# Projecting two heads through a block-diagonal omega instead of two row-packed halves

## The chip, the cores and the metric

The kernel runs on one core of a Trainium2 chip. The metric is the device time of one execution in microseconds (us), lower is better. A profile of one execution lists every instruction of the five engines: TensorE as two rows, PE for matmuls and PEld for the weight loads that go with them, VectorE (DVE), ScalarE (ACT), GpSimd (POOL) and SyncE (SP), which issues most DMAs. In the trace a matmul in full fp32 stands as two records (96 matmuls of a line give 192 records), one in fp32r as one record. The end of a matmul record is modelled, so blocks are measured here from start to start.

## What is computed

Random-feature attention on 4 batches, 8 heads, 576 tokens of 64 channels, 128 features, followed by a mixture of four experts:

```python
def phi(x):
    proj = np.einsum('bhsd,md->bhsm', x, omega)
    sq = np.sum(x * x, axis=-1, keepdims=True) / 2.0
    h = proj - sq
    h = h - np.max(h, axis=-1, keepdims=True)
    return np.exp(h) / np.sqrt(m)
q_p, k_p = (phi(q_s), phi(k_s))
kv = np.einsum('bhsm,bhsd->bhmd', k_p, v)
z = np.sum(k_p, axis=2)
num = np.einsum('bhsm,bhmd->bhsd', q_p, kv)
den = np.einsum('bhsm,bhm->bhs', q_p, z)[..., None] + 1e-06
x = num / den                              # 2304 tokens of 512 channels
for e in range(4):
    out += p[:, e:e + 1] * (np.maximum(x @ w1[e], 0.0) @ w2[e])
```

## The kernel before

One core does everything in one program whose order is written out by hand. Batch 0 is attended first (`class Pair`). The experts' work is cut into visits (a part of the tokens with half an expert): `plain` visits, then `fast` visits, which save products by sums and differences of blocks. While TensorE works through visits, the attention of batches one to three is fed in between in small ticks (`later_ticks`): 12 pairs of heads, each an object of `class Halves`. The last eight visits (`DEEP`) save products in the second layer too (`sevens`).

A pair of heads has its keys in one SBUF tile `k` of 128 partitions by 2 by 576: half 0 (`t[:, 0]`) holds the keys transposed, channels of head 0 on partitions 0 to 63 and of head 1 on 64 to 127; half 1 (`kn`) holds the same keys by tokens, which POOL squares in place (`square`, L251) and DVE sums to lengths (`lengths`, L255). Queries go the same way in a tile `q`. `om_r` holds omega transposed and scaled, 64 by 128, once for each head: on partitions 0 to 63 and again on 64 to 127.

`project` (L266) makes the features of 512 of the 576 tokens. For each of four groups of 128 tokens it does one matmul per head: the tokens are the stationary operand, 64 partitions by 128 columns, omega the moving one, 64 by 128. The two heads use different halves of the array's rows, and write to different PSUM banks (`ps[0]`, `ps[1]`). `project_tails` (L274) does the same for the last 64 tokens of each head, one matmul per head, to two banks more. Then come the row maxima (`maxima`, `maxima_tails`), the bias, and the exponentials on ACT. `sum_keys` multiplies the keys' features by the values: nine matmuls over the full array in fp32, one with 256 moving columns (L310) and eight with 128 (L314). `turn` transposes the queries' features (L325, L329), `numerators` (L353 to L355) applies the sums.

PSUM has eight banks, given out in turn by `bank`. In the `DEEP` visits `start_sides2` begins the work on the next visit's second-layer weights: four additions on POOL (L547 to L550, tile `w2f`). For the first `DEEP` visit it stands inside `sevens`, behind the splitting of `r11` on POOL (L956, then L502 `t_hl<-r`).

Of the kernel before, what the change touches and what calls it, by code (L numbers as in the profile page):

```python
# [6 lines left out]
F32 = mybir.dt.float32  # L7
F32R = mybir.dt.float32r
AF = mybir.ActivationFunctionType
ALU = mybir.AluOpType  # L10
AX = mybir.AxisListType
# [3 lines left out]
def attention_moe(ctx, tc, kT, qT, kd, qd, kn, qn, vn, omT, probs, w1, w2, out):  # L15
# [10 lines left out]
    nc = tc.nc  # L26
    _, NP, D, _ = kT.shape
    B, S = vn.shape[:2]
    M = omT.shape[1]
    NT, DM = out.shape  # L30
    E, FP, P, _ = w1.shape
# [9 lines left out]
    const = ctx.enter_context(tc.tile_pool(name="const", bufs=1))  # L41
# [24 lines left out]
    def bank(name):  # L66
        return psum.tile([P, 512], F32, tag="ps", name=name)
# [3 lines left out]


    om = const.tile([P, M], F32, name="om")
    om_r = const.tile([P, M], F32, name="om_r")
    ident = const.tile([P, P], F32, name="ident")
    pr = const.tile([P, NT // P, E], F32, name="pr")
    prs = const.tile([P, NT // P], F32, name="prs")
# [1 line left out]
    va = const.tile([P, 4, VZ], F32, name="va")  # L79
# [24 lines left out]
    H = 2 * P  # L104

    def held(shape, tag, dtype=F32R, name=None):
        return moe.tile(shape, dtype, tag=tag, name=name or tag, bufs=BUFS[tag])
# [5 lines left out]
    class Pair:  # L113
# [7 lines left out]
        def load(self, which, eng=nc.sync):  # L121
            src = {"k": kT, "q": qT}[which[0]][self.b, self.hp][:, TILES[int(which[1])]]
            t = xop([P, src.shape[1]], which, F32)
            setattr(self, which, t)
            eng.dma_start(t[:D], src)
# [28 lines left out]
        def exp(self, which, g):  # L154
            ps, nm = getattr(self, f"{which}h{g}")
            n = len(GROUPS[g])
            size = "t" if n == 1 else ""
            if which == "k" and n > 1 or which == "q" and g == 0:
                f = held([P, n, M], "hh" if which == "k" else "hl", F32, which + "p")
            else:  # L160
                f = att.tile([P, n, M], F32, tag=which + "p" + size, name=which + "p", bufs=2)
            for i in range(n):
                nc.scalar.activation(f[:, i], ps[:, i * P:(i + 1) * P], AF.Exp, bias=nm[:, i:i + 1])
            (self.kp if which == "k" else self.qx)[g] = f
# [73 lines left out]
    class Halves(Pair):  # L238
# [4 lines left out]
        def load(self, which):  # L243
            t = att.tile([P, 2, S], F32, tag=which, name=which, bufs=1)
            for i, (name, src) in enumerate(((which, {"k": kd, "q": qd}), (which + "n", {"k": kn, "q": qn}))):
                setattr(self, name, t[:, i])
                nc.sync.dma_start(t[:, i], src[which][self.b - 1, self.hp])

        def square(self, which):
# [8 lines left out]
        def project(self, which):  # L258

            t = getattr(self, which)  # L260
            ps = [bank(which + "_ps") for _ in range(2)]
            setattr(self, which + "_ps", ps)
            for i in range(4):
                for j in range(2):
                    rows, c = slice(j * D, (j + 1) * D), i * P + (1 - j) * D
                    nc.tensor.matmul(ps[j][:, i * P:(i + 1) * P], t[rows, c:c + P], om_r[rows], start=True, stop=True)  # L266

        def project_tails(self, which):
            self.t_ps = [bank("t_ps") for _ in range(2)]
            for x in ("mx", "nb"):  # L270
                setattr(self, x + which, att.tile([P, 9], F32, tag=x + which, name=x + which))
            for j in range(2):
                rows, cs = slice(j * D, (j + 1) * D), slice(j * (S - P), j * (S - P) + P)
                nc.tensor.matmul(self.t_ps[j][:, :M], getattr(self, which)[rows, cs], om_r[rows], start=True, stop=True)  # L274

        def maxima(self, which):
            mx, ps = getattr(self, "mx" + which), getattr(self, which + "_ps")
            for j in range(2):
                nc.vector.tensor_reduce(mx[:, 4 * j:4 * j + 4], ps[j].rearrange("p (i m) -> p i m", m=M), AX.X, ALU.max)

        def maxima_tails(self, which):
            for j in range(2):
                rows = slice(j * D, (j + 1) * D)
                nc.vector.tensor_reduce(getattr(self, "mx" + which)[rows, 8:], self.t_ps[j][rows, :M], AX.X, ALU.max)

        def bias(self, which):

# [1 line left out]
            nc.vector.scalar_tensor_tensor(mx, sq, -QS * QS / 2, mx, ALU.mult, ALU.add)  # L289
            nc.vector.scalar_tensor_tensor(nb, sq, -QS * QS / 2, mx, ALU.mult, ALU.subtract)  # L290

        def exp(self, which, j):
            ps, nb = getattr(self, which + "_ps")[j], getattr(self, "nb" + which)
            f = att.tile([P, 4, M], F32, tag=which + "p", name=which + "p", bufs=2)
            for i in range(4):
                nc.scalar.activation(f[:, i], ps[:, i * P:(i + 1) * P], AF.Exp, bias=nb[:, 4 * j + i:4 * j + i + 1])
            (self.kp if which == "k" else self.qx)[j] = f

        def exp_tails(self, which):
            f = att.tile([P, 1, M], F32, tag=which + "pt", name=which + "p", bufs=2)  # L300
            for j in range(2):
                rows = slice(j * D, (j + 1) * D)
                nc.scalar.activation(f[rows, 0], self.t_ps[j][rows, :M], AF.Exp, bias=getattr(self, "nb" + which)[rows, 8:])
            (self.kp if which == "k" else self.qx)[2] = f

        def sum_keys(self):


            kv = bank("kv")[:, :VZ]
            nc.tensor.matmul(kv, self.kp[2][:, 0], vb[:, self.hp], start=True, stop=False)  # L310
            for j in range(2):
                cs = slice((1 - j) * P, (2 - j) * P)
                for t in range(4):
                    nc.tensor.matmul(kv[:, cs], self.kp[j][:, t], va[:, t, cs], start=False, stop=(j == 1 and t == 3))  # L314
            self.kv_h, self.kv_l = (att.tile([P, VZ], F32R, tag=x, name=x, bufs=1) for x in ("kvh", "kvl"))
            nc.scalar.activation(self.kv_h, kv, AF.Copy, scale=1.0 / M)
            nc.vector.scalar_tensor_tensor(self.kv_l, kv, 1.0 / M, f32(self.kv_h), ALU.mult, ALU.subtract)

        def turn(self, part):

            n = 2 * P + part * D
            ps = bank("qt_ps")
            for j in range(2):
                for t in range(2):
                    nc.tensor.transpose(ps[:, (2 * j + t) * P:(2 * j + t + 1) * P], self.qx[j][:, 2 * part + t], ident)  # L325
            pieces = [(ps.rearrange("p (j t) -> p j t", j=2), slice(0, 2 * P))]
            if part:
                pt = bank("qt_ps")[:, :P]
                nc.tensor.transpose(pt, self.qx[2][:, 0], ident)  # L329
                pieces.append((pt.rearrange("p (j t) -> p j t", j=2), slice(2 * P, 2 * P + D)))  # L330
            qt_h, qt_l = (
                att.tile([P, 2, n], F32R, tag=f"{x}1" if part else "qt", name=x, bufs=2 - part) for x in ("qth", "qtl")
            )
            for src, cs in pieces:
                nc.scalar.activation(qt_h[:, :, cs], src, AF.Copy)
                nc.vector.tensor_tensor(qt_l[:, :, cs], src, f32(qt_h[:, :, cs]), ALU.subtract)
            if part == 0:
                self.qt = {}
            self.qt[part] = qt_h, qt_l
# [134 lines left out]
    DEEP = range(N0 + NV, len(visits))  # L474
# [22 lines left out]
    def split(t, a, c, hi, lo):  # L497
        if hi is nc.scalar:
            hi.activation(a, t, AF.Copy)  # L499
        else:  # L500
            hi.tensor_copy(a, t)
        lo.tensor_tensor(c, t, f32(a), ALU.subtract)  # L502
# [294 lines left out]
    def start_sides2(v):  # L797
        B = {}
        g = w2_sides(v, B)
        next(g)  # L800
        sides2[v] = B, g
# [5 lines left out]
    def fast(v):  # L807
# [119 lines left out]
        def sevens():  # L927
# [32 lines left out]
            for q in QS3:  # L960
                seventh(q, X[q][:, R], sums_of(5), mixed(1, R), start=False)
            split(r11, *T[7], nc.scalar, nc.gpsimd)
            if v == DEEP[0]:
                start_sides2(v + 1)
            next(ready, None)
            less(t1[:, 0], first_rows(P_[1]["p1"]), t2[:, 0])
            for q in QS3:
# [16 lines left out]
            ps = bank("g2")  # L984
# [62 lines left out]
        if deep:  # L1047
            less(t1[:, 1], last_rows(P_[0]["p5"]), r11[:, 1])
            p6(1)
            split(t1, *T[5], nc.scalar, nc.gpsimd)  # L1050
            next(ready, None)
            yield from sevens()
            return
# [26 lines left out]
    def begin():  # L1080
# [6 lines left out]
        ps = [Pair(0, hp) for hp in range(NP)]  # L1087
# [17 lines left out]
        def ones_b(t):  # L1105
            nc.gpsimd.memset(t, 0.0)
            nc.gpsimd.memset(t[:D, :, P + D:], 1.0)
            nc.gpsimd.memset(t[D:, :, :D], 1.0)
# [4 lines left out]

        ones_a(va)
        ones_b(vb)
        ps[0].load_tails()
        ps[1].load_v()
        scale_om()
# [56 lines left out]
        for p in ps:  # L1175
            p.load("q1")
        for j in range(2):
            nc.sync.dma_start(om_r[j * D:(j + 1) * D], omT)

        keys_exp(3)  # L1180
        ps[2].sum_keys()
# [181 lines left out]
```

## Time and profile before

| what | value |
|---|---|
| median of 3 runs | 897.58 us (897.53 to 898.04) |
| the profiled execution | 896.99 us, of which the span from first to last instruction is 895.2 us |
| PE, PEld, DVE, ACT, POOL busy | 99%, 89%, 65%, 53%, 59% of the span |
| chain that ended last | 94% PE |
| TensorE clock granted | 1.00 throughout |
| fp32 projections L266 and L274 | 384 and 96 records in 24 blocks (12 pairs, keys and queries), 83.7 to 521 us |

The profiled execution is 0.6 us below the median, so a difference found in its rows is added to the median as it is. The busy shares name PE as the engine to look at. A busy PE is not yet a PE at its peak: it matters which records follow each other at which distance, and whether something was waited for in between.

### The profile page before, as it was taken

To read this page: it belongs to the slowest core of one execution; us is meant where nothing else is said; L and a number is where in the kernel's file an instruction comes from. 1 tells how busy PE (TensorE), PEld (TensorE's weight loads), DVE (VectorE), ACT (ScalarE), POOL (GpSimd) and SP (SyncE) were. 2 spreads that over 40 slices of the span, in tenths; PEclk is the share of its full clock that TensorE was granted. 3 is DMA by queue.
4 is the path that set the end of the run, shared out by engine and by line. 5 is a ranking of instruction groups with operands and counts; after the bars stand their busy time and mean duration, and the time that the engine had idled before them with its cause. 6 is when DMAs were issued, how large, how long until landed. Compare 5 with 4: busy or idle time off the path is not lost.

```text
span 895.2 us, 14533 instructions
## 1 busy us (share of the span) xinstructions
PE 886.4 (99%) x5340; PEld 792.5 (89%) x5340; DVE 577.5 (65%) x985; ACT 478.2 (53%) x1077; POOL 532.1 (59%) x476
## 2 busy tenths in 40 slices
PE   9999999999999999999999999999999999999998
PEld 8888888888888888889888889888989999999998
DVE  5655566776768655574766564776756856856757
ACT  5454677676774555545455445454444544544541
POOL 4756365555634453343444333558889889898883
PEclk9999999999999999999999999999999999999999
DMA  7674454444522634234334413165333334234212
GB/s 181 161 213 141 136 159 136 152 149 136 179 63 59 237 93 171 83 118 142 135 111 149 143 63 141 60 198 202 125 110 128 121 103 144 89 125 155 81 59 83
DMA packets 57447, 117.21 MB, mean 131 GB/s; under 512 B 9824, under 2 KB 19744, under 8 KB 57376
## 3 DMA queue, kind: packets, MB, share of 16 engines
q1 hardware_dynamic: 52528, 99.21, 35.0%
q0 software_dynamic: 4608, 16.78, 5.4%
q8 instruction: 42, 0.69, 0.3%
q10 hardware_dynamic: 240, 0.30, 0.1%
q14 instruction: 29, 0.24, 0.1%
HBM read 94.77 MB, written 21.50 MB: 130 GB/s over the span
## 4 chain that ended last, share of the span: by engine, by line
PE 94%; DVE 3%; POOL 1%; issue 1%; DMA 1%; ACT 1%; SPq 0%; DVEq 0%; ACTq 0%
PE g L853 28%; PE g L925 13%; PE g L680 10%; PE g L682 10%; PE g L681 10%; PE g L665 3%; PE g L667 3%; PE g L666 3%; PE kv L314 2%; PE q_ps L266 1%; PE k_ps L266 1%; PE qt_ps L325 1%; PE nd L353 1%; PE k_ps L148 1%; PE kv L178 1%; PE nd L355 1%
## 5 line engine op out<-in xcount | busy, mean ns | idle before, releaser
L502 POOL TENSOR_TENSOR w2l<-w2r,w2h 128x512 fp32r<-128x512 f32 x93 | 121.5, 1316 | 106.3 <-ACT w2h L499 77.3
L699 DVE SCALAR_TENSOR_TENSOR acc<-g,pr,acc 128x256 f32<-128x256 f32 (+1 forms) x219 | 126.4, 604 | 46.2 <-PE g L682 31.7
L680 PE MATMUL g<-w2h,hh 128*128 128x512 f32 x344 | 137.5, 400 | 0.2 <-DVE hl L672 0.2
L682 PE MATMUL g<-w2h,hl 128*128 128x512 f32 x344 | 134.6, 391 | 0.8 <-DVE hl L672 0.8
L681 PE MATMUL g<-w2l,hh 128*128 128x512 f32 x344 | 134.4, 391 | 0.0
L875 DVE SCALAR_TENSOR_TENSOR hl<-sum,hh 128x448 fp32r<-128x448 f32 (+1 forms) x96 | 62.2, 650 | 97.0 <-ACT hh L871 96.2
L502 POOL TENSOR_TENSOR w1al<-w1r,w1ah 128x256 fp32r<-128x256 f32 (+1 forms) x77 | 82.6, 1090 | 55.2 <-ACT w1ah L499 46.4
L502 POOL TENSOR_TENSOR w1sl<-w1r,w1sh 128x512 fp32r<-128x512 f32 (+1 forms) x43 | 74.4, 1730 | 68.4 <-ACT w1sh L499 56.7
L866 DVE TENSOR_TENSOR sum<-g,sum 128x448 f32<-128x448 f32 x96 | 59.4, 621 | 66.7 <-PE g L853 66.4
L871 ACT ACTIVATE hh<-sum 128x448 fp32r<-128x448 f32 (+1 forms) x96 | 50.2, 524 | 92.3 <-DVE sum L866 92.3
L853 PE MATMUL g<-xbh,w1sh 128*128 128x448 f32 x256 | 93.8, 366 | 0.0
L853 PE MATMUL g<-xbl,w1sh 128*128 128x448 f32 x256 | 93.6, 366 | 0.0
L853 PE MATMUL g<-xbh,w1sl 128*128 128x448 f32 x256 | 93.5, 365 | 0.0
L859 ACT ACTIVATE sum<-g 128x448 f32<-128x448 f32 x96 | 51.6, 540 | 64.7 <-PE g L853 61.3
L682 PEld LDWEIGHTS g<-w2h,hl 128*128 128x128 f32 x344 | 64.6, 188 | 15.7 <-DVE hl L672 1.2
L680 PEld LDWEIGHTS g<-w2h,hh 128*128 128x128 f32 x344 | 64.7, 188 | 12.9 <-DVE hl L672 0.4
L681 PEld LDWEIGHTS g<-w2l,hh 128*128 128x128 f32 x344 | 64.7, 188 | 11.2
L853 PE MATMUL g<-xbh,w1ah 128*128 128x448 f32 x192 | 70.6, 368 | 0.0
L853 PE MATMUL g<-xbh,w1al 128*128 128x448 f32 x192 | 70.2, 366 | 0.0
L853 PE MATMUL g<-xbl,w1ah 128*128 128x448 f32 x192 | 70.1, 365 | 0.0
L499 ACT ACTIVATE w2h<-w2r 128x512 fp32r<-128x512 f32 x90 | 55.0, 627 | 23.5 <-DMA w2r<-in_w 11.7
L925 PE MATMUL g<-w2s,t_hl 128*128 128x256 f32 x432 | 55.2, 281 | 0.0
(198 smaller groups left out, 2207.6 us busy)
## 6 DMA issues: line engine op xcount, KB each, us to landing
w1r<-in_w SPq DMA_DIRECT2D x54, 512.0 KB, 3.7
w2r<-in_w SPq DMA_DIRECT2D x108, 256.0 KB, 2.8
kept<-w1sh SPq DMA_DIRECT2D x16, 512.0 KB, 4.6
kept<-w1sl SPq DMA_DIRECT2D x16, 512.0 KB, 5.5
w1sh<-kept POOLq DMA_DIRECT2D x16, 512.0 KB, 4.3
w1sl<-kept POOLq DMA_DIRECT2D x16, 512.0 KB, 5.1
va<-in_vn SPq DMA_DIRECT2D x14, 256.0 KB, 4.6
k<-in_kd SPq DMA_DIRECT2D x12, 288.0 KB, 4.1
```

The lines of the kernel that those rows point to most:

```text
L499: hi.activation(a, t, AF.Copy)
L502: lo.tensor_tensor(c, t, f32(a), ALU.subtract)
L680: nc.tensor.matmul(ps, ha[:, ts_], wa, start=(c == 0), stop=False)
L681: nc.tensor.matmul(ps, ha[:, ts_], wc, start=False, stop=False)
L682: nc.tensor.matmul(ps, hc[:, ts_], wa, start=False, stop=(c == FH - 1))
L699: nc.vector.scalar_tensor_tensor(acc[i][:, cs], ps, sc, acc[i][:, cs], ALU.mult, ALU.add)
L853: nc.tensor.matmul(ps, a[:, w], x[:, k], start=(start and k + at == 0), stop=(k == 1 and at == 2), skip_group_check=not start)
L859: nc.scalar.activation(t, P_[g][where], AF.Copy)
L866: nc.vector.tensor_tensor(t, P_[g][where], t, ALU.add)
L871: nc.scalar.activation(ha, t, AF.Relu)
L875: nc.vector.scalar_tensor_tensor(x, y, 0.0, f32(z), ALU.max, ALU.subtract)
L925: nc.tensor.matmul(to, x, w, start=(start and f + k == 0), stop=(f + k == 3), skip_group_check=not start)
```

## The change

Three things are changed.

1. `om_r` becomes 128 by 256, zero off the diagonal: head 0's omega on partitions 0 to 63 and columns 0 to 127, head 1's on partitions 64 to 127 and columns 128 to 255. POOL zeroes it once at the start, the same two DMAs fill it. `project` does one matmul for both heads per group of 128 tokens: stationary 128 partitions by 128 columns, moving 128 by 256. The heads' features of a group stand side by side, two groups to a bank; maxima and exponentials read them there, with as many instructions of as many elements as before. The host no longer rolls the tokens of even heads by 64.
2. The tails of both heads go to one bank. Each tail matmul now takes all 128 partitions and a window of 128 columns of the flattened tile, so that the 64 wanted rows come out on the head's own partitions: for head 0 the last 64 tokens and the first 64 columns of `kn`, for head 1 the last 128 tokens. The other 64 rows that come out are not read.
3. For the first `DEEP` visit, `start_sides2` of the next visit is called earlier, ahead of `sevens`.

```diff
-    om_r = const.tile([P, M], F32, name="om_r")
+    om_r = const.tile([P, 2 * M], F32, name="om_r")
...
             for i in range(4):
-                for j in range(2):
-                    rows, c = slice(j * D, (j + 1) * D), i * P + (1 - j) * D
-                    nc.tensor.matmul(ps[j][:, i * P:(i + 1) * P], t[rows, c:c + P], om_r[rows], start=True, stop=True)
+                o = i % 2 * 2 * M
+                nc.tensor.matmul(ps[i // 2][:, o:o + 2 * M], t[:, i * P:(i + 1) * P], om_r, start=True, stop=True)
...
-            self.t_ps = [bank("t_ps") for _ in range(2)]
+            ps = bank("t_ps")
+            self.t_ps = [ps[:, j * M:(j + 1) * M] for j in range(2)]
...
-                rows, cs = slice(j * D, (j + 1) * D), slice(j * (S - P), j * (S - P) + P)
-                nc.tensor.matmul(self.t_ps[j][:, :M], getattr(self, which)[rows, cs], om_r[rows], start=True, stop=True)
+                cs = slice(S - (1 + j) * D, S - (1 + j) * D + P)
+                nc.tensor.matmul(self.t_ps[j], getattr(self, which + "all")[:, cs], om_r[:, j * M:(j + 1) * M], start=True, stop=True)
...
-            for j in range(2):
-                nc.vector.tensor_reduce(mx[:, 4 * j:4 * j + 4], ps[j].rearrange("p (i m) -> p i m", m=M), AX.X, ALU.max)
+            to = mx[:, :8].rearrange("p (j i) -> p i j", j=2)
+            for h in range(2):
+                nc.vector.tensor_reduce(to[:, 2 * h:2 * h + 2], ps[h].rearrange("p (i j m) -> p i j m", j=2, m=M), AX.X, ALU.max)
...
             split(r11, *T[7], nc.scalar, nc.gpsimd)
-            if v == DEEP[0]:
-                start_sides2(v + 1)
...
             split(t1, *T[5], nc.scalar, nc.gpsimd)
+            if v == DEEP[0]:
+                start_sides2(v + 1)
...
+        nc.gpsimd.memset(om_r, 0.0)
```

On PE, at the projection of the second pair's keys (with the semaphores waited for: `DMAHW` a DMA, `Pool`, `DVE` and `Activation` an engine). Before:

```order
L682 MATMUL g_1385<-w2h,hl 128x512
L266 MATMUL k_ps<-om_r,k 128x128 [waits DMAHW7_49]
L266 MATMUL k_ps<-om_r,k 128x128 x7
L274 MATMUL t_ps<-om_r,k 128x128 [waits DVE_49] x2
L353 MATMUL nd<-qth,kvh 128x256 [waits DVE_49,Activation_49]
```

and after, where a count is of matmuls and sizes are of their outputs:

```order
L687 MATMUL g_1376<-w2h,hl 128x512
L266 MATMUL k_ps<-om_r,k 128x256 [waits DMAHW7_49]
L266 MATMUL k_ps<-om_r,k 128x256 x3
L276 MATMUL t_ps<-om_r,k 128x128 [waits DVE_49,Pool_49]
L276 MATMUL t_ps<-om_r,k 128x128
L358 MATMUL nd<-qth,kvh 128x256 [waits DVE_49]
```

Eight matmuls of 128 columns became four of 256, at the same place; the two tails stay two of 128, and the first of them waits for POOL as well.

On POOL, in the first `DEEP` visit (`w2f` are the sums of the next visit's second-layer weights, `r` is `r11`, the DMAs fetch first-layer weights). Before:

```order
L502 TENSOR_TENSOR t_hl<-va,t_hl 128x768
L632 DMA w1sh<-kept 128x1024
L632 DMA w1sl<-kept 128x1024
L956 TENSOR_TENSOR r_6651<-vb,r_6651 128x768
L502 TENSOR_TENSOR t_hl<-r_6651,t_hl 128x768
L547 TENSOR_TENSOR w2f<-w2r 128x256
L548 TENSOR_TENSOR w2f<-w2f,w2r 128x256
L549 TENSOR_TENSOR w2f<-w2r,w2f 128x256
L550 TENSOR_TENSOR w2f<-w2r 128x256
L502 TENSOR_TENSOR w1al<-w1r,w1ah 128x512
```

and after:

```order
L507 TENSOR_TENSOR t_hl<-va,t_hl 128x768
L552 TENSOR_TENSOR w2f<-w2r 128x256
L553 TENSOR_TENSOR w2f<-w2f,w2r 128x256
L554 TENSOR_TENSOR w2f<-w2r,w2f 128x256
L555 TENSOR_TENSOR w2f<-w2r 128x256
L637 DMA w1sh<-kept 128x1024
L637 DMA w1sl<-kept 128x1024
L961 TENSOR_TENSOR r_6532<-vb,r_6532 128x768
L507 TENSOR_TENSOR t_hl<-r_6532,t_hl 128x768
L507 TENSOR_TENSOR w1al<-w1r,w1ah 128x512
```

The four additions moved ahead of two DMA issues and two operations on `r`. Apart from these places, and one more memset on POOL near the start, every engine's instructions stand in the same order.

## Rows read from the trace of the kernel before

**Rows 1.** The page: busy time of each engine, share, instructions.
```profile
PE 886.4 (99%) x5340; PEld 792.5 (89%) x5340; DVE 577.5 (65%) x985; ACT 478.2 (53%) x1077; POOL 532.1 (59%) x476
```

**Rows 2.** Busy us by stretch, after its length: PE, PEld, DVE, ACT, POOL; PEclk.
```profile
83.00:260.00 177.00, 176.22 (x1190) 151.03 (x1189) 117.69 (x202) 124.82 (x331) 95.89 (x83) 1.00 0.45 142
...
320.00:530.00 210.00, 210.00 (x1133) 182.37 (x1133) 128.55 (x219) 107.00 (x240) 81.79 (x66) 1.00 0.36 124
```

**Rows 3.** PE's waits: who waited for whom, us in total, times, longest.
```profile
PE g L925 <- DVE hl L908: 1.0, 1, 1.0
PE g L682 <- DVE hl L672: 0.8, 1, 0.8
```

**Rows 4.** Lines L266 and L274, keys: count, duration ns min/median/max, first and last start.
```profile
L266 PE MATMUL k_ps<-om_r,k x192: 272/272/373, 83.7 to 495.3; 64*128 64x128 f32 x192
...
L274 PE MATMUL t_ps<-om_r,k x48: 272/272/272, 84.7 to 495.5; 64*128 64x128 f32 x48
```

**Rows 5.** PE's timeline around one projection: start, us, line, operation, array used, count.
```profile
88.55 0.39 PE L665 MATMUL g<-xh,w1sh 128*128 128x512 f32 x1
...
89.00 0.39 PE L667 MATMUL g<-xh,w1sl 128*128 128x512 f32 x1
89.32 1.16 PE L266 MATMUL q_ps<-om_r,q 64*128 64x128 f32 x16
90.32 0.39 PE L274 MATMUL t_ps<-om_r,q 64*128 64x128 f32 x4
90.64 0.50 PE L665 MATMUL g<-xh,w1ah 128*128 128x512 f32 x1
90.97 0.39 PE L666 MATMUL g<-xl,w1ah 128*128 128x512 f32 x1
```

**Rows 6.** PE's timeline around one sum of keys.
```profile
95.53 0.39 PE L665 MATMUL g<-xh,w1sh 128*128 128x512 f32 x1
...
95.98 0.39 PE L667 MATMUL g<-xh,w1sl 128*128 128x512 f32 x1
96.21 0.59 PE L310 MATMUL kv<-vb,kp 128*128 128x256 f32 x2
96.64 1.95 PE L314 MATMUL kv<-va,kp 128*128 128x128 f32 x16
98.34 0.47 PE L680 MATMUL g<-w2h,hh 128*128 128x512 f32 x1
98.66 0.39 PE L681 MATMUL g<-w2l,hh 128*128 128x512 f32 x1
```

**Rows 7.** POOL's timeline in the first deep visit; in brackets, idle before and its releaser.
```profile
627.07 1.86 POOL L502 TENSOR_TENSOR t_hl<-va,t_hl 128x768 fp32r<-128x768 f32 x1 [2.54 <-ACT t_hl L499]
628.87 0.57 POOL L632 DMA_DIRECT2D w1sh<-kept  x1
...
632.42 1.86 POOL L956 TENSOR_TENSOR r<-vb,r 128x768 f32<-128x768 f32 x1 [2.45 <-DVE vb L837]
635.24 2.04 POOL L502 TENSOR_TENSOR t_hl<-r,t_hl 128x768 fp32r<-128x768 f32 x1 [0.96 <-ACT t_hl L499]
637.24 0.73 POOL L547 TENSOR_TENSOR w2f<-w2r 128x256 f32<-128x256 f32 x1
...
640.26 1.99 POOL L502 TENSOR_TENSOR w1al<-w1r,w1ah 128x512 fp32r<-128x512 f32 x2
...
643.31 1.99 POOL L502 TENSOR_TENSOR hl<-va,hh 128x384 fp32r<-128x384 f32 x2
```

**Rows 8.** PE's timeline behind that visit's `hl`.
```profile
644.74 0.28 PE L925 MATMUL g<-w2l,hh 128*128 128x256 f32 x1
645.36 0.39 PE L925 MATMUL g<-w2h,hl 128*128 128x256 f32 x1 [0.34 <-POOL hl L502]
```

**Rows 9.** SP's timeline: issue of that visit's last second-layer weights.
```profile
617.09 5.25 SPq L495 DMA_DIRECT2D w2r<-in_w  x3
```

**Rows 10.** The page, DMA issues: count, KB each, median us to landing.
```profile
w2r<-in_w SPq DMA_DIRECT2D x108, 256.0 KB, 2.8
```

**Rows 11.** Timelines of POOL and PE: a square of keys, and the tails that follow.
```profile
238.72 1.15 POOL L251 TENSOR_TENSOR k<-k 128x576 f32<-128x576 f32 x1
...
241.59 0.39 PE L274 MATMUL t_ps<-om_r,k 64*128 64x128 f32 x4
```

More of the change, by code (lines that the diff above doesn't have):

```diff
@@ L246, in load @@
                 setattr(self, name, t[:, i])
+                setattr(self, which + "all", t.rearrange("p i s -> p (i s)"))
                 nc.sync.dma_start(t[:, i], src[which][self.b - 1, self.hp])
@@ L283, in maxima_tails @@
                 rows = slice(j * D, (j + 1) * D)
-                nc.vector.tensor_reduce(getattr(self, "mx" + which)[rows, 8:], self.t_ps[j][rows, :M], AX.X, ALU.max)
+                nc.vector.tensor_reduce(getattr(self, "mx" + which)[rows, 8:], self.t_ps[j][rows], AX.X, ALU.max)
         def bias(self, which):
@@ L290, in bias, with exp @@
             nc.vector.scalar_tensor_tensor(nb, sq, -QS * QS / 2, mx, ALU.mult, ALU.subtract)
-        def exp(self, which, j):
-            ps, nb = getattr(self, which + "_ps")[j], getattr(self, "nb" + which)
+        def exp(self, which, h):
+            ps, nb = getattr(self, which + "_ps")[h], getattr(self, "nb" + which)
             f = att.tile([P, 4, M], F32, tag=which + "p", name=which + "p", bufs=2)
-            for i in range(4):
-                nc.scalar.activation(f[:, i], ps[:, i * P:(i + 1) * P], AF.Exp, bias=nb[:, 4 * j + i:4 * j + i + 1])
-            (self.kp if which == "k" else self.qx)[j] = f
+            for i in range(2):
+                for j in range(2):
+                    o, c = (2 * i + j) * M, 4 * j + 2 * h + i
+                    nc.scalar.activation(f[:, 2 * j + i], ps[:, o:o + M], AF.Exp, bias=nb[:, c:c + 1])
+            (self.kp if which == "k" else self.qx)[h] = f
         def exp_tails(self, which):
@@ L302, in exp_tails @@
                 rows = slice(j * D, (j + 1) * D)
-                nc.scalar.activation(f[rows, 0], self.t_ps[j][rows, :M], AF.Exp, bias=getattr(self, "nb" + which)[rows, 8:])
+                nc.scalar.activation(f[rows, 0], self.t_ps[j][rows], AF.Exp, bias=getattr(self, "nb" + which)[rows, 8:])
             (self.kp if which == "k" else self.qx)[2] = f
@@ L313, in sum_keys @@
                 for t in range(4):
-                    nc.tensor.matmul(kv[:, cs], self.kp[j][:, t], va[:, t, cs], start=False, stop=(j == 1 and t == 3))
+                    nc.tensor.matmul(kv[:, cs], self.key_tile(j, t), va[:, t, cs], start=False, stop=(j == 1 and t == 3))
             self.kv_h, self.kv_l = (att.tile([P, VZ], F32R, tag=x, name=x, bufs=1) for x in ("kvh", "kvl"))
@@ L324, in turn @@
                 for t in range(2):
-                    nc.tensor.transpose(ps[:, (2 * j + t) * P:(2 * j + t + 1) * P], self.qx[j][:, 2 * part + t], ident)
+                    nc.tensor.transpose(ps[:, (2 * j + t) * P:(2 * j + t + 1) * P], self.query_tile(j, 2 * part + t), ident)
             pieces = [(ps.rearrange("p (j t) -> p j t", j=2), slice(0, 2 * P))]
@@ L1177, in begin @@
         for j in range(2):
-            nc.sync.dma_start(om_r[j * D:(j + 1) * D], omT)
+            nc.sync.dma_start(om_r[j * D:(j + 1) * D, j * M:(j + 1) * M], omT)
         keys_exp(3)
@@ L1325, in halves @@
     def halves(x):
-        t = x.transpose(0, 1, 3, 2).copy()
-        t[:, ::2] = np.roll(t[:, ::2], D, -1)
-        return t.reshape(-1, H // 2, 2 * D, S)
+        return x.transpose(0, 1, 3, 2).reshape(-1, H // 2, 2 * D, S)
     def rows(x):
```

## The prediction

> **What bounds the kernel now.** I read the page's busy times first: PE is busy for 99% of the span, the next engine, DVE, for 65% [rows 1]. The stretches then say whether this also holds where the projections lie, from 83.7 to 521 us [rows 4]: PE is busy for 176.2 of 177 us and for 210.0 of 210 us, at a granted clock of 1.00, the 2.4 GHz level [rows 2]. The waits of PE say what an edit on another engine could bring at most: behind the first 50 us the two longest are 1.0 us on DVE's `hl` of L908 and 0.8 us on `hl` of L672, each once [rows 3]. So TensorE's own stream sets the end, and the question is how long that stream's blocks are, before and after. Since the ends of matmul records are modelled, I measure each block from the start of the matmul ahead of it to the start of the second matmul behind it, and take off two ordinary steps. In that way whatever it costs to go into a block and out of it is counted.
>
> **The projections, what goes.** The block runs from the g matmul at 89.00 to the second one behind it at 90.97, 1.97 us [rows 5]. An ordinary step is half of 88.55 to 89.00, 0.225 us, so the block costs 1.97 - 0.45 = 1.52 us. What is in it: 20 records on half of the array's rows each (64 partitions, as the rows show), 16 of which start within 1.00 us (89.32 to 90.32), 0.0625 us each. Two half-height records thus take hardly more than one full-height one of the same width (0.11 us, next paragraph): the halves work side by side. Had every pair of records taken 0.112 us, the block would be 10 x 0.112 = 1.12 us. The other 0.40 us is entering and leaving the half-height form: 89.00 to 89.32 is 0.32 us where a step is 0.225, and 90.64 to 90.97 is 0.33 us.
>
> The Trainium skill has this as a rule, in TensorEngine Tiling (Array Packing), section Key Properties: a change of tiling mode drains TensorE. The block's edges agree with it. It is the one rule that speaks for the change, and 24 x 0.40 = 9.6 us is what it could give if nothing were paid for it.
>
> **The projections, what comes.** The trace of before has the very form that replaces them, on the full array, in `sum_keys` [rows 6]: two records of 128x256 in fp32, at 96.21 and up to 96.64, so 0.43 / 2 = 0.215 us each; then 16 records of 128x128. The whole block, measured as above, is 95.98 to 98.66, 2.68, less 95.53 to 95.98, 0.45, makes 2.23 us. Less 0.43 this leaves 1.80 / 16 = 0.112 us for each record of 128 columns. With these two prices the block adds up without a rest, so fp32 on the full array costs nothing on the way in or out. A record of 256 columns costs 1.9 times one of 128.
>
> After the change a block has 4 matmuls of 256 columns, 8 records, and 2 tails of 128 columns, 4 records: 8 x 0.215 + 4 x 0.112 = 1.72 + 0.45 = 2.17 us. So each block grows by 2.17 - 1.52 = 0.65 us. The zeros of the block-diagonal omega are multiplied like any number; the gain at the edges, 0.40, is less than the side-by-side work that is given up: 0.83 on the main matmuls (1.72 less 8 x 0.112) and 0.22 on the tails (0.45 less 2 x 0.112). There are 24 blocks (12 pairs, keys and queries; the 192 records of L266 for keys are 12 x 16 [rows 4]): 24 x 0.65 = +15.6 us, all on PE's stream, which in these stretches has 0.8 us of idle time in 387 [rows 2].
>
> **Maxima, exponentials, banks.** As many instructions of as many elements as before, on DVE and ACT, which are far from the bound [rows 2]; a block takes three banks instead of four. I cost this at nothing: PE's stream gets longer by 0.65 us per block, which is cover for them. The first bank is also complete half a block before the second, so the first maximum can start while PE still projects. That could shorten the 0.8 us wait on L672 [rows 3], which follows a projection. Bounds: 0 to -0.8 us; I take 0, since one wait in 24 blocks shows that it needs a coincidence.
>
> **The tails' new wait.** Head 0's tail now reads columns that POOL squares, so PE waits for the square, and behind it in PE's queue stands all further work. In the tightest place that I found, the square of keys runs from 238.72 to 239.87, the tails come at 241.59: 1.7 us to spare [rows 11]. The main matmuls put 1.72 us ahead of the tails instead of 1.00, which adds 0.7. I cost it at nothing; bounds 0 to what a rival below says.
>
> **`om_r`.** One more memset on POOL near the start and a scaling of 256 columns instead of 128 on DVE: no place on PE's path, below 0.3 us, taken as 0.
>
> **`start_sides2` earlier.** The four additions span 637.24 to 640.26, 3.0 us. In front of them POOL idles for 2.45 us before L956 (for DVE's `vb`) and 0.96 before `t_hl` [rows 7]. Moved behind `t_hl<-va` they run from 628.9 to 631.9; their inputs were issued by 622.3 (617.09 + 5.25) [rows 9] and land 2.8 us later [rows 10], at about 625, so they wait for nothing. The two DMA issues behind them end at 633.0 instead of 630.0, L956 starts at 633.0 instead of 632.42, `t_hl<-r` 0.6 us later, and the `w1al` behind at 637.8 instead of 640.26: POOL is 2.4 us ahead from there. Then `hl<-va` is done 2.4 us earlier than the 645.3 for which PE stands still: the step from 644.74 to 645.36 is 0.62 us where its neighbours take 0.12 [rows 8]. That stall, 0.5 us, goes. What is late next is DVE's `hl` (1.0 us [rows 3]), which lies in the same visit's successor; POOL running ahead may shift it. Bounds for this part: 0 to -1.5; I take -0.5. The first-layer weights arrive 3 us later for the next visit, a whole visit ahead of their use.
>
> **The sum.** +15.6 - 0.5 = +15.1 us. On the profiled execution (896.99) that is 912.1, on the median 897.58 + 15.1 = 912.7 us.
>
> **The rivals.** (a) *Packing was worth nothing, its edges were the cost.* If a record of 256 columns took the 0.112 us of one of 128, a block would be 12 x 0.112 = 1.34 us, 0.18 less than before, 24 x 0.18 = 4.3 us, and with the stall 897.58 - 4.3 - 0.5 = 892.8 us: faster. The point from which it decides: 8r + 0.45 = 1.52, r = 0.134 us per record of 256 columns. For it speaks that fp32r records of 256 columns step at 0.12 us [rows 8]; against it, that the operands here are fp32, and the only fp32 records of 256 columns took 0.215 [rows 6]. I give it 4%. The Trainium skill's TensorE: Matmul & The Clock Gate, section Back-to-back issue gap, has the same outcome: N/2.4 + 2.5 ns, 109 ns for 256 columns, without a word on the type. By that figure, as an estimate, the blocks would be 24 x 0.20 = 4.8 us shorter in all; the fp32 rows do not agree with it.
>
> (b) *PE's slack swallows it.* The longer blocks would have to replace waits; there are 0.8 us of them in 387 [rows 2]. A result within 0.2%, about 898, needs 15 us of waits: 3%.
>
> (c) *Partly given back.* Both DVE waits [rows 3] go too, 0.8 + 1.0: 912.7 - 1.8 = 910.9 us, 13%.
>
> (d) *The tails wait for POOL.* If POOL falls behind by more than the 1.7 us [rows 11], all of PE waits. If the square only began when the tails are due, each of 12 key blocks would cost one square, 1.15 us: 12 x 1.15 = 13.8, 926.5 us. POOL is busy for only 54% of the first stretch (95.9 of 177) and 39% of the second [rows 2]: 4%.
>
> (e) *Half of the edges stays.* If half of the 0.40 us came from changing between fp32r and fp32, and not from the half-height form, the new blocks would pay it too: 24 x 0.20 = +4.8, 917.5 us. The sum of keys stands between fp32r matmuls just so and shows no such cost [rows 6]: 4%.
>
> **How the numbers follow.** My forecast, 912.7 us, gets 72%. The range has to take in (c), the rounding of the rows (0.02 us per block, 0.5 us in all) and small waits that I priced at nothing: 909.5 to 916.0 us; (a), (b), (d) and (e), 15%, lie outside it. About 0.2% of the time, 1.8 us, is what a measurement of this kernel can tell from no change. Faster is (a), 4%; the same is (b), 3%; slower is the rest, 93%.
>
> **What would show it.** In the profile after, two records of the new L266 should start 0.215 us apart, 0.43 us per matmul, and a block, edges off, should be 2.17 us instead of 1.52; the first g matmul behind the tails should step like that at 98.34 [rows 6]. PE's idle time should stay under 1% and the clock at 1.00. The stall at 645.36 should be gone, POOL's `w1al` some 2.4 us earlier against PE. I am wrong if the records of 256 columns step at 0.134 us or less, if PE waits at the tails for POOL's square, or if the granted clock falls.

## The result and the profile after

The changed kernel takes 910.42 us (median of 4 runs, 909.57 to 911.49) against 897.56 for the kernel before on the same chip: +12.9 us, a ratio of 1.0145 with a 95% interval of 1.0128 to 1.0163. It is slower, as forecast, and 2.3 us less than the predicted 912.7. On a second chip it took 909.94 against 896.82, +13.1 us, ratio 1.0146 (1.0132 to 1.0160).

The profiled execution took 911.49 us with a span of 909.7. The page shows the same bound as before [rows 1], with 16 us more of it on PE and 21 on PEld, 192 PE records fewer, and the busy times of DVE, ACT and POOL unchanged to 3 us:

```profile
PE 902.7 (99%) x5148; PEld 813.6 (89%) x5148; DVE 580.4 (64%) x985; ACT 478.7 (53%) x1077; POOL 533.6 (59%) x477
```

The two stretches of the projections (length, then PE, PEld, DVE, ACT, POOL busy, granted clock), to be held against [rows 2]. PE has 0.15 us of idle time in 402, and the clock is at 1.00, the 2.4 GHz level:

```profile
83.00:275.00 192.00, 191.85 (x1090) 168.69 (x1089) 124.11 (x207) 128.06 (x336) 96.73 (x85) 1.00 0.43 132
335.00:545.00 210.00, 210.00 (x1045) 184.79 (x1045) 124.09 (x210) 106.02 (x238) 79.34 (x64) 1.00 0.36 121
```

PE's timeline around the projection that [rows 5] show of before (start, us, line, operation, array used, count):

```profile
89.33 0.39 PE L670 MATMUL g<-xh,w1sh 128*128 128x512 f32 x1
...
89.79 0.39 PE L672 MATMUL g<-xh,w1sl 128*128 128x512 f32 x1
90.02 1.89 PE L266 MATMUL q_ps<-om_r,q 128*128 128x256 f32 x8
91.74 0.61 PE L276 MATMUL t_ps<-om_r,q 128*128 128x128 f32 x4
92.10 0.48 PE L670 MATMUL g<-xh,w1ah 128*128 128x512 f32 x1
92.42 0.40 PE L671 MATMUL g<-xl,w1ah 128*128 128x512 f32 x1
```

The eight records run from 90.02 to 91.74, 0.215 us each, as predicted. The block is entered after 0.23 us (89.79 to 90.02), an ordinary step, where it took 0.32 before. Behind the tails the first g matmul steps by 0.32 us (92.10 to 92.42), as at 98.34 in [rows 6]. From 89.79 to 92.42 it is 2.63 us; two ordinary steps off (89.33 to 89.79, 0.46), 2.17 us. Measured in the same way, each of the 24 blocks is 0.65 to 0.67 us longer than its counterpart before.

PE's waits (who for whom, us in total, times, longest). The 0.8 us on `hl` of L672 in [rows 3] is down to 0.2 (L677 now), and the waits on `hl` of L913 are two, at other places:

```profile
PE g L930 <- DVE hl L913: 1.1, 2, 0.6
...
PE g L687 <- DVE hl L677: 0.2, 1, 0.2
```

The wait of [rows 8] on POOL's `hl` is gone; the same matmul now follows the one ahead of it by 0.12 us:

```profile
660.22 0.28 PE L930 MATMUL g<-w2l,hh 128*128 128x256 f32 x1
660.34 0.28 PE L930 MATMUL g<-w2h,hl 128*128 128x256 f32 x1
```

### The profile page after: what moved, and what is told of

Its sections match the earlier page's. It is cut to its first block, busy times and chain, and to the rows that moved or that the text cites. A ratio compares the mean times of both kernels' runs of the same rounds, so it can differ in the third digit from the quotient of the medians.

```text
span 909.7 us, 14154 instructions
## 1 busy us (share of the span) xinstructions
PE 902.7 (99%) x5148; PEld 813.6 (89%) x5148; DVE 580.4 (64%) x985; ACT 478.7 (53%) x1077; POOL 533.6 (59%) x477
## 4 chain that ended last, share of the span: by engine, by line
PE 92%; DVE 4%; issue 1%; POOL 1%; ACT 1%; DMA 1%; SPq 0%; POOLq 0%; ACTq 0%; DVEq 0%
PE g L858 27%; PE g L930 11%; PE g L687 9%; PE g L685 9%; PE g L686 9%; PE g L670 3%; PE g L672 3%; PE g L671 3%; PE kv L319 2%; PE q_ps L266 2%; PE k_ps L266 2%; PE qt_ps L330 1%; PE t_ps L276 1%; DVE hl L880 1%; PE k_ps L148 1%
## 5 line engine op out<-in xcount | busy, mean ns | idle before, releaser
L687 PEld LDWEIGHTS g<-w2h,hl 128*128 128x128 f32 x344 | 64.6, 188 | 15.1 <-DVE hl L677 0.6
```

Of the source, the lines that this page charges most:

```text
L687: nc.tensor.matmul(ps, hc[:, ts_], wa, start=False, stop=(c == FH - 1))
```

## The experiments

The theory was: TensorE's stream sets the end; a block of the new form costs its columns, 0.65 us more than the half-height blocks with their edges, 24 times; the earlier `start_sides2` gives a little back. The rivals: the gain falling short of the sum comes out of the projections; what is costly is the 256-column form or the tails; the move of `start_sides2` does nothing.

### The projections alone, and `start_sides2` alone

First the changed kernel with the third change undone:

```diff
             split(t1, *T[5], nc.scalar, nc.gpsimd)
-            if v == DEEP[0]:
-                start_sides2(v + 1)
...
             split(r11, *T[7], nc.scalar, nc.gpsimd)
+            if v == DEEP[0]:
+                start_sides2(v + 1)
```

> The changed kernel with start_sides2 back in its old place; so the block-diagonal projections and shared tails alone. Theory (the projections' columns set the time: a block of 2.17 us instead of 1.52, 24 blocks, +15.6 us; the earlier call of start_sides2 gives back about 1 us by removing PE's waits at 645 and 661 us): 912 to 914 us, one half to 2 us above the changed kernel. Rival (the 2.7 us by which the measured difference falls short of 15.6 come from the projections themselves, for instance from waits that the longer blocks cover): the same time as the changed kernel within 0.5 us.

913.05 us against 896.96: +16.1 us, ratio 1.0177 (1.0163 to 1.0190).

Then the kernel before with the third change alone (the same diff, the other way round, on the kernel before):

> The kernel before with start_sides2 called earlier and nothing else. Theory (the move takes away PE's waits near 645 and 661 us): 0.5 to 2 us faster than the kernel before, so 895.5 to 897 us, and the waits on DVE's hl at 661 us gone from the profile. Rival (those waits come and go between executions and the move does nothing): the same as before, 897.6 us within 0.5.

895.25 us against 896.96: -1.7 us, ratio 0.9978 (0.9969 to 0.9986). It is faster than both kernels. What became of PE's waits is not what I had argued. The wait behind POOL's `hl` [rows 8] went, as predicted, and so did the wait on DVE's `hl` near 662, which in the kernel before looks like this on PE's timeline:

```profile
662.72 0.38 PE L925 MATMUL g<-w2h,hl 128*128 128x256 f32 x1 [1.04 <-DVE hl L908]
```

But a new one came at 633.90. Here are PE, POOL and DVE of the version with the move alone:

```profile
633.90 0.39 PE L925 MATMUL g<-w2h,hl 128*128 128x256 f32 x1 [0.46 <-DVE hl L908]
```

```profile
628.80 0.73 POOL L547 TENSOR_TENSOR w2f<-w2r 128x256 f32<-128x256 f32 x1
629.61 1.00 POOL L548 TENSOR_TENSOR w2f<-w2f,w2r 128x256 f32<-128x256 f32 x1
```

```profile
628.88 1.14 DVE L875 SCALAR_TENSOR_TENSOR hl<-sum,hh 128x448 fp32r<-128x448 f32 x1 [0.65 <-ACT hh L871]
629.94 1.09 DVE L837 SCALAR_TENSOR_TENSOR vb<-sum,va 128x384 f32<-128x384 f32 x1
```

and the same two DVE operations in the kernel before, where POOL only issued DMAs beside them:

```profile
628.97 0.62 DVE L875 SCALAR_TENSOR_TENSOR hl<-sum,hh 128x448 fp32r<-128x448 f32 x1 [0.64 <-ACT hh L871]
629.51 0.55 DVE L837 SCALAR_TENSOR_TENSOR vb<-sum,va 128x384 f32<-128x384 f32 x1
```

So DVE's operations take 0.5 us longer each where POOL's additions run beside them; that puts `hl` about 1 us later, and PE waits. Following the same matmuls through both traces, the move costs 0.6 us at 633, gives back 0.7 by 645 and 1.5 at 661 to 663, 1.5 us in all. At 661 DVE's chain, now 1.6 us earlier (its L908 at 660.41 instead of 662.05), no longer keeps PE waiting. Of these 1.6 us, 0.9 are one operation, in the kernel before

```profile
658.64 1.22 DVE L875 SCALAR_TENSOR_TENSOR hl<-sum,hh 128x64 fp32r<-128x64 f32 x1 [0.97 <-ACT hh L871]
```

and with the move

```profile
657.59 0.35 DVE L875 SCALAR_TENSOR_TENSOR hl<-sum,hh 128x64 fp32r<-128x64 f32 x1 [0.45 <-ACT hh L871]
```

Before, all of it but the last 0.08 us lay beside POOL's splitting of `w2s` (658.47 to 659.78); with the move, 0.27 us of it does (POOL's splitting ends at 657.86). As the rows read, more than half of the gain at 661 is thus the same lengthening as the loss at 633, avoided this time by the new order.

Both kernels ran once more on one chip, since 16.1 - 1.7 = 14.4 is more than the 12.9 measured for the change as a whole:

> The changed kernel once more, on the same chip as the next, to part its two effects. Theory (blocks +16 us, earlier start_sides2 -1.7 us, as measured each alone): 14 to 14.5 us above the kernel before of this chip. Rival (the two together give something that neither gives alone): below 13 us, as the first comparison of 12.9 us suggests.

> The changed kernel with start_sides2 in its old place, once more on the same chip. Theory: 15.6 to 16.2 us above the kernel before, 1.7 above the changed kernel. Rival: 2.5 us or more above the changed kernel.

Measured against 896.82: the changed kernel 909.94, +13.1 us (ratio 1.0146, 1.0132 to 1.0160); the projections alone 911.86, +15.0 us (1.0171, 1.0157 to 1.0185). The theory's 14 to 14.5 was too high, but it was the +16.1 that was high: on this chip the blocks cost 15.0 and the move gives 1.9 back. All intervals hold a sum of 15.3 - 1.8 = 13.5, so the times show no effect that only both together have. The profiles say the same: the 24 blocks move the matmuls behind them by the same 15.4 us in all four profiles of the two kernels, and the move gives 1.5 us with the new blocks and without. The second profile of the changed kernel is 12.9 us longer than that of before; the first, 14.5, loses 0.8 us at 781 in a wait that the second lacks, and ends its first 80 us 0.5 us later.

### Which part of the block costs what

The tails half-height again, in two banks:

```diff
-            ps = bank("t_ps")
-            self.t_ps = [ps[:, j * M:(j + 1) * M] for j in range(2)]
+            self.t_ps = [bank("t_ps")[:, :M] for _ in range(2)]
...
-                nc.tensor.matmul(self.t_ps[j], getattr(self, which + "all")[:, cs], om_r[:, j * M:(j + 1) * M], start=True, stop=True)
+                rows = slice(j * D, (j + 1) * D)
+                nc.tensor.matmul(self.t_ps[j], getattr(self, which + "all")[rows, cs], om_r[rows, j * M:(j + 1) * M], start=True, stop=True)
```

> The changed kernel, but the tails done as before, one half-height matmul per head, side by side, to two banks; the main matmuls stay block-diagonal. Theory (half-height pairs cost 0.112 us per pair of records, and any passage into and out of the half-height form 0.40 us): a block of 1.72 + 2 x 0.112 + 0.40 = 2.34 us, 24 x 0.17 = 4 us slower than the changed kernel, about 914.5 us. Rival (the tails' halves side by side are worth what they save, 0.22 us, and the edges cost nothing by themselves): 24 x 0.22 = 5 us faster than the changed kernel, about 905 us.

914.28 us, +17.3 on before (ratio 1.0196, 1.0182 to 1.0210), 3.9 above the changed kernel's first median, 4.2 to 4.4 by the differences to the kernel before (expected 4). Its block on PE's timeline, where the tails stand on 64 rows:

```profile
82.74 0.39 PE L672 MATMUL g<-xh,w1sl 128*128 128x512 f32 x1
82.97 1.89 PE L266 MATMUL k_ps<-om_r,k 128*128 128x256 f32 x8
84.79 0.49 PE L276 MATMUL t_ps<-om_r,k 64*128 64x128 f32 x4
85.21 0.50 PE L670 MATMUL g<-xh,w1sh 128*128 128x512 f32 x1
85.55 0.39 PE L671 MATMUL g<-xl,w1sh 128*128 128x512 f32 x1
```

82.74 to 85.55 less 0.45 is 2.36 us, predicted 2.34. Of it the matmuls are 1.72 + 0.22, so the edges of the half-height form are 0.41 us even around four records.

The other way round, the main matmuls half-height, the tails full:

```diff
-                o = i % 2 * 2 * M
-                nc.tensor.matmul(ps[i // 2][:, o:o + 2 * M], t[:, i * P:(i + 1) * P], om_r, start=True, stop=True)
+                for j in range(2):
+                    rows = slice(j * D, (j + 1) * D)
+                    nc.tensor.matmul(ps[j][:, i * P:(i + 1) * P], t[rows, i * P:(i + 1) * P], om_r[rows, j * M:(j + 1) * M], start=True, stop=True)
```

(maxima and exponentials read the heads' banks as in the kernel before)

> The changed kernel, but the main matmuls done as before, one half-height matmul per head, side by side, to two banks; the tails stay full-height in one bank. Theory: a block of 8 x 0.112 + 0.40 + 4 x 0.112 = 1.74 us, 0.22 above the kernel before and 0.43 below the changed kernel: 24 x 0.43 = 10.4 us faster than the changed kernel, about 900 us; the slowing is 0.22 x 24 = 5 us for the tails and 10 us for the main matmuls. Rival (the tails with their wait for POOL's square carry the loss): as slow as the changed kernel, 910 us.

900.33 us, +3.4 on before (ratio 1.0039, 1.0024 to 1.0054). Its block:

```profile
82.98 0.39 PE L670 MATMUL g<-xh,w1sl 128*128 128x512 f32 x1
83.30 1.16 PE L267 MATMUL k_ps<-om_r,k 64*128 64x128 f32 x16
84.39 0.71 PE L277 MATMUL t_ps<-om_r,k 128*128 128x128 f32 x4
84.86 0.48 PE L668 MATMUL g<-xh,w1sh 128*128 128x512 f32 x1
85.18 0.39 PE L669 MATMUL g<-xl,w1sh 128*128 128x512 f32 x1
```

82.98 to 85.18 less 0.45 is 1.75 us, predicted 1.74. Entering takes 0.32 us again. The tails carry 24 x 0.23 = 5.5 us of the loss (less the 1.8 of the move, which this kernel has too: 3.7, measured 3.4), the main matmuls the rest. It also tells something of the wait on `hl` at 254 (0.8 us in [rows 3], 0.15 in the changed kernel): with the heads' banks as before it is 0.52.

```profile
257.08 0.50 PE L685 MATMUL g<-w2h,hl 128*128 128x512 f32 x1 [0.52 <-DVE hl L675]
```

### What a matmul costs

Every main matmul twice:

```diff
-                nc.tensor.matmul(ps[i // 2][:, o:o + 2 * M], t[:, i * P:(i + 1) * P], om_r, start=True, stop=True)
+                for _ in range(2):
+                    nc.tensor.matmul(ps[i // 2][:, o:o + 2 * M], t[:, i * P:(i + 1) * P], om_r, start=True, stop=True)
```

> The changed kernel with every block-diagonal main matmul done twice into the same place (the second overwrites the first with the same numbers). Theory (TensorE's stream sets the end; each matmul of 256 fp32 columns costs two records of 0.215 us): 96 matmuls more of 0.43 us each, 24 x 4 x 0.43 = 41.3 us slower than the changed kernel, about 952 us. Rival (part of a block is waiting, for which a second matmul would be free): clearly less than 35 us slower.

951.86 us against 897.58, +54.3; that is 41.4 more than the changed kernel's +12.9, expected 41.3. No part of a block is waiting for which a further matmul would be free.

The 256 columns in two pieces:

```diff
-                o = i % 2 * 2 * M
-                nc.tensor.matmul(ps[i // 2][:, o:o + 2 * M], t[:, i * P:(i + 1) * P], om_r, start=True, stop=True)
+                for j in range(2):
+                    o = (i % 2 * 2 + j) * M
+                    nc.tensor.matmul(ps[i // 2][:, o:o + M], t[:, i * P:(i + 1) * P], om_r[:, j * M:(j + 1) * M], start=True, stop=True)
```

> The changed kernel with every main matmul cut into two of 128 moving columns, one per head, over the full array; the same columns in all, twice as many matmuls and weight loads. Theory (a record's price goes by its columns: 0.112 us for 128, 0.215 for 256): a block of 16 x 0.112 + 4 x 0.112 = 2.24 us, 24 x 0.07 = 1.7 us slower than the changed kernel, about 912 us. Rival (what is new and costly is the 256-column form, not the work on zeros): a block near 1.5 us and a time near the kernel before, 898 us.

911.69 us against 897.58, +14.1 (ratio 1.0160, 1.0146 to 1.0174). PE's timeline:

```profile
83.06 0.39 PE L673 MATMUL g<-xh,w1sl 128*128 128x512 f32 x1
83.29 1.95 PE L267 MATMUL k_ps<-om_r,k 128*128 128x128 f32 x16
85.07 0.61 PE L277 MATMUL t_ps<-om_r,k 128*128 128x128 f32 x4
85.44 0.48 PE L671 MATMUL g<-xh,w1sh 128*128 128x512 f32 x1
85.75 0.40 PE L672 MATMUL g<-xl,w1sh 128*128 128x512 f32 x1
```

16 records from 83.29 to 85.07, 0.111 us each: the same sixteen records that on half of the rows took 1.00 us [rows 5] take 1.78 on all of them. It is the row packing that is lost, not the form of 256 columns that is dear. In time it comes to 1.3 us more than the changed kernel's first median, expected 1.7; medians from two chips hardly tell that from nothing; the block lengths (2.24 against 2.17) do.

And fp32 against fp32r (the keys and queries of 512 tokens are left out of the projection, as the expectation says):

```diff
+    om_f = const.tile([P, M], F32R, name="om_f")
...
-                nc.tensor.matmul(ps[i // 2][:, o:o + 2 * M], t[:, i * P:(i + 1) * P], om_r, start=True, stop=True)
+                nc.tensor.matmul(ps[i // 2][:, o:o + 2 * M], om_f, om_f[:, None, :].to_broadcast([P, 2, M]), start=True, stop=True)
```

> The changed kernel with the main matmuls fed in fp32r from a small tile of rounded omega, as stationary and as moving operand; the keys and queries of the 512 tokens are left out of the projection, so only its time means something. Theory (what makes 256 columns cost 0.215 us is fp32, not the full array or the 256 columns): one record instead of two per matmul, 0.12 us apart, a block of 4 x 0.12 + 4 x 0.112 = 0.93 us, 24 x 1.24 = 30 us faster than the changed kernel, about 881 us. Rival (a full-height matmul of 256 columns between fp32 tails costs 0.2 us whatever its type): a block of 4 x 0.215 + 0.45 = 1.31 us, about 890 us.

882.09 us against 897.58 (ratio 0.9831, 0.9818 to 0.9844), 28.3 below the changed kernel, expected 30. PE's timeline:

```profile
83.79 0.39 PE L673 MATMUL g<-xh,w1sl 128*128 128x512 f32 x1
84.02 0.63 PE L267 MATMUL k_ps<-om_f 128*128 128x256 f32 x4
84.49 0.60 PE L277 MATMUL t_ps<-om_r,k 128*128 128x128 f32 x4
84.85 0.48 PE L671 MATMUL g<-xh,w1sh 128*128 128x512 f32 x1
85.17 0.40 PE L672 MATMUL g<-xl,w1sh 128*128 128x512 f32 x1
```

Four records from 84.02 to 84.49, 0.117 us each, one per matmul: the block is 0.93 us. In fp32 the same matmul takes 0.43, 3.7 times as long.

### Where to put the four additions, and DVE's reciprocal

The move one step further, ahead of the splitting of `t1`, in the kernel before:

```diff
+            if v == DEEP[0]:
+                start_sides2(v + 1)
             split(t1, *T[5], nc.scalar, nc.gpsimd)
-            if v == DEEP[0]:
-                start_sides2(v + 1)
```

> The kernel before with start_sides2 called one step earlier than in the change, ahead of the splitting of t1, so that its four additions run on POOL from about 624.5 us, where POOL waits for ACT. Theory (POOL's additions slow DVE's operations that run beside them, 1.1 us instead of 0.6 each, and what DVE is late with PE waits for): the wait of 0.6 us near 633 us that the move brought goes or shrinks, and another may come near 626 us; 894.5 to 896 us, level with the moved version within 0.7. Rival (any place ahead of the DMA issues is as good, the time is set elsewhere): the same waits as in the moved version.

895.66 us against 897.58 (ratio 0.9983, 0.9974 to 0.9992), level with the move of the change (-1.7). The wait at 633 went and one of its size came ahead of it, again behind DVE's `hl`:

```profile
626.28 0.39 PE L925 MATMUL g<-w2h,hl 128*128 128x256 f32 x1 [0.57 <-DVE hl L908]
```

Last, the reciprocal in front of the wait at 254 us [rows 3], on top of the move alone:

```diff
             p.bias("q")
-            if before:
-                before.invert(1)
             yield
             p.exp_tails("q")
             p.exp("q", 0)
             if before:
+                before.invert(1)
                 before.times(1)
```

> The kernel before with the earlier start_sides2 and DVE's second reciprocal of a pair (2.15 us) issued one tick later, behind the features' bias and the next relu. PE's wait of 0.9 us at 253 us stands behind that reciprocal. Theory (the wait follows DVE's order there): the wait at 253 goes, 0.5 to 0.9 us below the version with the earlier start_sides2 alone, about 2.5 us below the kernel before. Rival (DVE's time is only shifted to another wait): the same as the moved version within 0.4 us.

894.57 us against 896.82: -2.25 us, ratio 0.9973 (0.9963 to 0.9984). PE's wait for `hl` of the first-layer relu, 0.8 us in [rows 3], stands nowhere in its list of waits any more, and the profiled span is 892.6 against 893.6 for the move alone. In its trace, all matmuls behind that place come 1.1 us earlier against those ahead of it than in the trace of the move alone. Against the move alone the medians, each beside its own kernel before, differ by 0.5 us, within the intervals of both; so the traces show that the wait is gone, but the times don't settle how much that brought beyond the move. It has the lowest median of all versions against its kernel before; the intervals of the three versions with a moved `start_sides2` and the old blocks overlap.

## Why the prediction was right, and where not

**The blocks.** The block before was read as 1.52 us, the one after predicted as 2.17 from rows of another part of the kernel; measured 2.17. 24 x 0.65 = 15.6 us were predicted; followed through the profiles, the matmuls behind the blocks come 15.4 us later (0.64 per block; 0.02 of what a block shows at its own edges comes back behind it). The kernel with this part alone took +16.1 and +15.0, which holds the shorter wait of the maxima too (below). The step that carried it was to price the new form by an existing fp32 block of the same width [rows 6] and not by fp32r matmuls of that width, which are everywhere in this kernel. The two runs with one half of the block in each form confirm all three prices: 0.112 per pair of half-height records, 0.215 per record of 256 columns, 0.40 for the edges.

Two readings on the way were weaker than they look. The prediction saw the leaving edge in the step of 0.33 us from 90.64 to 90.97; but behind full-height records this step is the same (98.34 to 98.66 in [rows 6], 92.10 to 92.42 after), so the step alone shows no edge. The two steps named there would also make only 0.2 of the 0.40 us. In [rows 5] entering costs 0.20 (0.32 instead of 0.225, then 16 records in 1.00 instead of 0.90 us), and leaving 0.20 (90.32 to 90.97, 0.65 us, where two pairs and a step are 0.45). The total was right, since the whole block had been measured. And that [rows 6] "adds up without a rest" showed nothing, as 0.112 had been found by dividing up that rest. It is the run with the columns in two pieces that shows it: there a record of 128 columns takes 0.111 us, measured inside the block.

The Trainium skill has the price of the type in FP8 and Floating Point Precision, section TensorE Precision Notes: true fp32 takes four passes through the array. As an estimate, 4 x 256 columns at 2.4 GHz are 0.427 us; the 0.43 us per matmul here agree, and so does fp32r with about a quarter. The 109 ns that rival (a) has from the Trainium skill (TensorE: Matmul & The Clock Gate, Back-to-back issue gap) would then be the price of one pass; an fp32r record took 117 ns here.

**The rivals.** (a), packing worth nothing, is out: the same 16 records took 1.00 us packed and 1.78 unpacked. (b), slack: PE had 0.8 us of it in those stretches before and 0.15 after. (c), both DVE waits given back, is closest to what was measured: its 910.9 us, with a chance of 13%, lies nearer to 910.4 than the forecast of 912.7. One of the two waits shrank from 0.8 to 0.15 us and the other went; but a new one of 0.46 came at 649, so it is in part luck that (c) hits the number so closely. (d), the tails waiting for POOL's square, did not occur: no idle time stands in front of the tails. In the tightest place of the profile after, the square ends at 177.64 and the tails start at 179.94, 2.3 us to spare where [rows 11] had 1.7:

```profile
176.49 1.15 POOL L252 TENSOR_TENSOR k<-k 128x576 f32<-128x576 f32 x1 [3.52 <-DMA k<-in_kn]
```

```profile
179.94 0.61 PE L276 MATMUL t_ps<-om_r,k 128*128 128x128 f32 x4
```

(e), half of the edges staying, is out: with it the block would be 2.37 us, and it is 2.17.

**The maxima, priced at 0 with a bound of -0.8.** It was -0.6. The chain of DVE behind the projection starts when the first bank is complete, half a block before the end now, and ends in `hl`, for which PE had waited. The run with half-height main matmuls, which keeps the heads' banks, has 0.26 us of this gain; so the order of the banks can be the cause of the other 0.37 only. That the full-height tails behind the main matmuls give DVE time for the 0.26 is likely, but no run has it alone. In the profile after that wait is 0.15 us:

```profile
264.05 0.50 PE L687 MATMUL g<-w2h,hl 128*128 128x512 f32 x1 [0.15 <-DVE hl L677]
```

**`start_sides2`, priced at -0.5.** It measured -1.7 alone and -1.9 in the changed kernel by the times, -1.5 by the profiles: mis-sized by 1 us or more, at or beyond the bound of -1.5 that I gave it. The 0.5 us at 645 went as said, and POOL ran 2.05 us ahead (2.4 predicted). What the step missed was DVE: I looked for idle time on POOL to put the additions in, and took their inputs and the DMAs behind them into account, but not that DVE works beside them. That brought a loss of 0.6 us at 633 which I had not foreseen, and it is also where the larger gain lies, 1.5 us at 661 to 663. The trace of before could have told: there DVE's L837 already took 0.55 us alone and up to 1.15 beside POOL (the lines stand in the last section).

**The sum.** Following the same matmuls through the profile of before and the second one of the changed kernel, the first 80 us give -0.4, the blocks +15.4, the wait at 254 -0.6 and the visit with the move -1.5: 12.9 us, the difference of the two spans; the times say 12.9 and 13.1. The forecast of +15.1 missed by 2 us: 0.6 in the maxima, 1.0 in `start_sides2`, 0.2 in the blocks; the rest is of the size by which the first 80 us differ from profile to profile (-0.8 to +0.1 us), and no run ties it to the change.

## What to carry to other kernels

A block-diagonal operand multiplies its zeros: it pays only when what it saves at the edges is more than the half of the array that it wastes, here 0.40 us against 1.05 per block. Price a new form by rows of the same type and width that the trace already has, edges included, from start to start; fp32 and fp32r of one shape differed 3.7 times. And where work is put into an engine's idle time, look at what the engines beside it are doing at that time, not at that engine alone.

## What the runs showed of the hardware that was not expected

POOL's additions of 128x256 in SBUF and DVE's operations with two operands in SBUF lengthened each other when they ran side by side: DVE from 0.62 to 1.14 us and from 0.55 to 1.09, POOL's L548 from 0.74 to 1.00. DVE's operations that read one operand from PSUM (`g`) kept their length. Here are some of them from the trace of before (duration in ns, min/median/max). No `vb<-sum,va` ran beside a computing operation of POOL; of `va<-sum,r` 14 of 16 did, of `va<-g,vb` all, of L866 40 of the 48 after 600 us:

```profile
L837 DVE SCALAR_TENSOR_TENSOR vb<-sum,va x16: 544/551/555, 629.5 to 877.3; 128x384 f32<-128x384 f32 x16
L837 DVE SCALAR_TENSOR_TENSOR va<-sum,r x16: 548/858/1151, 623.9 to 870.9; 128x384 f32<-128x384 f32 x16
L837 DVE SCALAR_TENSOR_TENSOR va<-g,vb x8: 548/549/552, 632.8 to 878.3; 128x384 f32<-128x384 f32 x8
L866 DVE TENSOR_TENSOR sum<-g,sum x96: 607/624/626, 296.1 to 875.5; 128x448 f32<-128x448 f32 x96
```

The Trainium skill's SBUF — State Buffer, section Terms, says that the two engines share a pair of ports of which one holds a lock for a whole instruction while the other is blocked. The trace roughly agrees: POOL's addition starts at 628.80 and ends at 629.53 after an undisturbed 0.73; DVE's operation, started at 628.88, ends at 630.02, 0.49 after POOL's end, where its ordinary length is 0.62. No run took the port alone away, so this cause is argued from the rows.

The other was that the edges of the half-height form cost the same, 0.40 to 0.41 us, around 4 records, 16 or 20.
